# The head of an attention-plus-MLP kernel: two instead of three column blocks row tile by row tile, and the rows of query block 2 loaded earlier

## The chip, the cores and the metric

The kernel runs on one core of a Trainium2 chip. The metric is the device time of one execution, in microseconds (us), as the median of several runs.

## The reference, cut to what matters

```python
def reference(A_x, A_k_cache, A_v_cache, A_wq, A_wo, B_x, B_W_gate, B_W_up, B_W_down):
    x = A_x                                   # (1, 2048, 512) bf16
    xn = _layernorm(x, axis=-1)
    s = _A_ref(xn, A_k_cache, A_v_cache, A_wq, A_wo)          # 32 heads of attention, 2048 keys
    g = _silu(_B_ref(xn, B_W_gate, B_W_up, B_W_down))         # relu(xn Wg) * (xn Wu), then Wd
    return x + s * g
```

The branch with gate, up and down weights (512 x 1792, and back) is computed first, in four query blocks of 512 rows. Each block has 14 column blocks of 128 ("block 0" to "block 13" below) and then a down projection of four row tiles of 128 rows. The attention follows. The change touches only query block 0, at the very start.

## The kernel before: the parts that the change and the argument touch

The loads at the start are all issued from one queue, SP, except two:

```python
FCS = [0, 2, 5, 9, FC]          # weight pieces: blocks 0-1, 2-4, 5-8, 9-13
HFC = 3                         # blocks computed row tile by row tile
load_x0(sp, 0); load_x0(act, 1)                 # rows of query block 0, one tile each
load_w(sp, Wg_sb, wg_src, sem_wg, 0); load_w(act, Wu_sb, wu_src, sem_wu, 0)
load_x0(sp, 2); load_x0(sp, 3)
load_w(sp, Wg_sb, wg_src, sem_wg, 1); load_w(sp, Wu_sb, wu_src, sem_wu, 1)
load_xq(1)                                      # 512 rows of query block 1
load_w(sp, Wg_sb, wg_src, sem_wg, 2); load_w(sp, Wu_sb, wu_src, sem_wu, 2)
load_w(sp, Wg_sb, wg_src, sem_wg, 3); load_w(sp, Wu_sb, wu_src, sem_wu, 3)
for Q in range(2, QB):
    load_xq(Q)
sem_wd.sig(sp.dma_start(Wd_sb[:], ...))
```

(Statements are joined on lines here, to save room.) The head centres the rows on VectorE, transposes them on TensorE into PSUM, lets ScalarE copy them to `xcT`, and multiplies each row tile as soon as it is there. `head_tile(n, fc)` is eight matmuls of 128 columns: row tile n times gate and up weights of block fc.

```python
def head_ln():
    c0 = head_transpose(0, head_center(0))
    warm_mm(4)                       # matmuls on constants, no use made of them
    c1 = head_transpose(1, head_center(1))
    n2 = head_center(2)
    n3 = head_center(3)
    _wait(pe, c0)                    # c0..c3: the copy of that row tile is done
    head_tile(0, 0)
    head_tile(0, 1)
    _wait(pe, c1)
    head_tile(1, 0)
    head_tile(1, 1)
    c2 = head_transpose(2, n2)
    head_tile(0, 2)                  # these two run while ScalarE copies row tile 2
    head_tile(1, 2)
    _wait(pe, c2)
    head_tile(2, 0)
    c3 = head_transpose(3, n3)
    head_tile(2, 1)
    head_tile(2, 2)                  # and these two while it copies row tile 3
    _wait(pe, c3)
    for fc in range(HFC):
        head_tile(3, fc)
```

Blocks from HFC on use 512 columns, four matmuls for gate and four for up. The first of them uses the two accumulator banks; the others use a ring of three PSUM slots. A slot comes free when VectorE has multiplied gate and up. After each block of query block 0, VectorE and ScalarE also do one piece of the layernorm of later rows:

```python
def finish_gate_up(Q, fc, s, gtok, gu_tok):
    ...
    rtok = sem_relu.sig(act.activation(gr_sb[gk][:], g_ps, ACTF.Relu))
    _wait(dve, gu_tok); _wait(dve, rtok)
    h_tok = sem_h.sig(dve.tensor_tensor(hT[par][:, fc, :], gr_sb[gk][:], u_ps, ALU.mult))
    ...
    if Q == 0:
        ln_task(fc)     # fc 0-3: statistics of query block 1; 4-7: of block 2; 8-11: of block 3;
                        # 13: rstd of block 0, r2, r2h
```

So `ln_task(4)`, right after the multiply of block 4, needs the rows of query block 2. `r2h`, the last thing of that VectorE chain, is the scale of the first Tanh of the down projection, whose gate result frees the PSUM bank for row tile 2:

```python
_wait(act, ytok)                     # row tile j of the down projection is done
_wait(act, sig_free[jb])
if Q == 0 and j == 0:
    _wait(act, ln_hold["r2"])
stok = sem_sig.sig(act.activation(sig_sb[jb][:], ps_acc[:, jb, 0:D], ACTF.Tanh,
                                  scale=r2h[:, j, 0:1] if Q == 0 else 0.5))
```

The softmax here doesn't subtract the row's maximum and nothing guards it: scores larger than these inputs give would overflow.

## Time and profile before

| | before |
|---|---|
| median, lowest and highest of the first three runs | 1286.01 us, 1285.67 to 1286.48 |
| span in the profile | 1284.4 us |
| PE busy | 1279.1 us |
| first row-tile matmul of the head | 6.28 us |
| block 3 starts | 12.18 us |
| down projection of query block 0 starts | 31.70 us |
| first matmul of query block 1 | 44.03 us |

The last four are starts read from the timeline of the PE. From the profile's page, parts 1 and 4 (busy time with its share of the span and the number of instructions; then the chain of work that ended last, by engine):

```profile
PE 1279.1 (100%) x12050; PEld 836.4 (65%) x12050; DVE 380.5 (30%) x683; ACT 1002.2 (78%) x1111; POOL 13.2 (1%) x25
PE 98%; DVE 1%; ACT 0%; issue 0%; DMA 0%; ACTq 0%; DVEq 0%
```

TensorE bounds the kernel. The next view, the windows of the kernel before, shows where the little that is left lies. Its columns are the stretch, its length, then the busy time and number of instructions of each engine:

```profile
6.28:12.18 5.90, 5.90 (x108) 5.82 (x106) 2.21 (x7) 2.68 (x5) 0.00 (x0) 1.00 1.10 343
12.18:31.70 19.52, 19.15 (x91) 8.54 (x89) 16.12 (x40) 6.60 (x15) 6.03 (x8) 1.00 1.07 259
31.70:44.03 12.33, 12.26 (x58) 5.40 (x57) 6.45 (x14) 4.22 (x7) 6.25 (x8) 1.00 0.64 134
44.03:144.00 99.97, 99.97 (x465) 45.34 (x464) 37.35 (x55) 30.54 (x51) 0.00 (x0) 1.00 0.14 26
...
```

The first number after the length is PE's. PE is without a gap in the head, lacks 0.37 us in the second stretch and 0.07 us in the third, and has none from 44.03 to 144 us (nor, in a further window, from 144 to 1270 us: 1126.00 of 1126.00 us). The record of four wide matmuls lasts 1.03 us, though the next four start 0.86 us after them when nothing holds them: a busy record reaches 0.17 us too far, so the true losses are larger: from start to start 0.53 us and 0.24 us. Both come from waits. Of the list of waits of the kernel before, up to 44.03 us, four (total, times, longest):

```profile
DVE stats L313 <- DMA x_sb<-in_A_x_dram: 4.3, 2, 3.5
ACT L539 <- DVE r2h L449: 2.1, 1, 2.1
PEld ps_acc L531 <- DVE g_sb L548: 0.6, 1, 0.6
PE ps_r L508 <- DVE hT L473: 0.4, 1, 0.4
```

And the timeline around 20 us (start, duration, instruction, and in brackets the idle time before it and what ended it), first VectorE:

```profile
18.16 0.69 DVE L473 TENSOR_TENSOR hT<-gr_sb,ps_r 128x512 bf16<-128x512 bf16 x1 [0.92 <-ACT gr_sb L467]
19.62 0.69 DVE L313 BATCH_NORM_STATS2 stats<-x_sb 128x6 f32<-128x512 bf16 x1 [0.78 <-DMA x_sb<-in_A_x_dram]
...
20.51 0.69 DVE L473 TENSOR_TENSOR hT<-gr_sb,ps_r 128x512 bf16<-128x512 bf16 x1
```

then PE, at the head and at block 8:

```profile
8.07 0.39 PE L358 MATMUL ps_acc<-ident,xc_sb 128*128 128x128 bf16 x4
8.29 0.39 PE L410 MATMUL ps_r<-xcT,Wg_sb 128*128 128x128 bf16 x4
...
12.18 1.03 PE L508 MATMUL ps_acc<-xcT,Wg_sb 128*128 128x512 bf16 x4
13.04 1.03 PE L512 MATMUL ps_acc<-xcT,Wu_sb 128*128 128x512 bf16 x4
...
21.34 1.02 PE L508 MATMUL ps_r<-xcT,Wg_sb 128*128 128x512 bf16 x4 [0.37 <-DVE hT L473]
```

VectorE finishes the multiply of block 4 at 18.85 us and stands until the rows of query block 2 land, at 19.62. The multiply of block 5 therefore ends at 21.2 instead of about 20.4, and PE block 8, which needs that slot, starts at 21.34 instead of 20.81. Last, the chain of waits in order of time shows how the same VectorE chain goes on into the down projection:

```profile
34.12 0.50 DVE r2h L449
...
34.69 1.28 ACT L539
...
35.99 0.69 ACT sig_sb L539
...
37.23 0.70 DVE g_sb L548
...
37.97 1.04 PE ps_acc L531 x4
```

Row tile 2 of the down projection (37.97) starts only when the first gate result (37.93) has freed its bank, and the table load ahead of the first Tanh (34.69) waited for `r2h`.

### The profile page before, as it was taken

Reading aid. Unit: us, or ns where it says so; the run is one execution under the profiler, and the core shown is the slowest. Engines: PE = TensorE matmul, PEld = TensorE weight load, DVE = VectorE, ACT = ScalarE, POOL = GpSimd, SP = SyncE. Lnnn points to the kernel's source line nnn. Section 1 sums busy time; section 2 is a strip of 40 time slices with the busy share of each in tenths; the row PEclk is TensorE's granted clock in tenths of the full one; section 3 lists DMA queues with packets and bytes.
Section 4 is the critical chain, followed back from the end, with each engine's and each line's share of the span. In section 5 each row is a group of like instructions: output and inputs, shape, how many; then the busy total and the mean of one; then the engine's idle time right before and its main releaser. Section 6 shows DMA issues by size and latency. Waiting matters only on the chain.

```text
span 1284.4 us, 26956 instructions
## 1 busy us (share of the span) xinstructions
PE 1279.1 (100%) x12050; PEld 836.4 (65%) x12050; DVE 380.5 (30%) x683; ACT 1002.2 (78%) x1111; POOL 13.2 (1%) x25
## 2 busy tenths in 40 slices
PE   9999999999999999999999999999999999999998
PEld 5444466676666666666666666666666666666665
DVE  6433311112222222222222222222222222224355
ACT  3322399998888888888888888888888888888885
POOL 2100000000000000000000000000000000000000
PEclk9999999999999999999999999999999999999999
DMA  9600123332132332332322322233323322332212
GB/s 262 131 1 1 22 46 57 58 55 38 35 54 46 71 54 50 55 70 51 55 43 33 67 46 54 55 66 55 55 51 65 58 35 38 51 67 54 48 16 75
DMA packets 242033, 72.13 MB, mean 56 GB/s; under 512 B 227840, under 2 KB 241920, under 8 KB 241920
## 3 DMA queue, kind: packets, MB, share of 16 engines
q1 hardware_dynamic: 241248, 70.02, 29.6%
q8 instruction: 96, 1.57, 0.5%
q10 hardware_dynamic: 672, 0.39, 0.1%
q14 instruction: 17, 0.14, 0.0%
HBM read 32.77 MB, written 2.10 MB: 27 GB/s over the span
## 4 chain that ended last, share of the span: by engine, by line
PE 98%; DVE 1%; ACT 0%; issue 0%; DMA 0%; ACTq 0%; DVEq 0%
PE ps_acc L769 36%; PE ps_r L664 34%; PE ps_r L597 9%; PE ps_r L618 8%; PE ps_acc L531 3%; PE ps_r L508 3%; PE ps_r L512 3%; PE ps_r L803 1%; DVE stats L313 0%; PE ps_r L410 0%; DVE hT L473 0%; DMA x_sb<-in_A_x_dram 0%; DVE fin_tmp L811 0%; ACT gr_sb L467 0%; DVE x_sb L827 0%
## 5 line engine op out<-in xcount | busy, mean ns | idle before, releaser
L674 ACT ACTIVATE PT<-ps_r 128x1024 bf16<-128x1024 f32 x1024 | 952.5, 1054 | 167.7 <-PE ps_r L664 167.7
L769 PEld LDWEIGHTS ps_acc<-V_sb,PT 128*128 128x128 bf16 x8192 | 621.2, 98 | 241.9 <-ACT PT L674 3.5
L769 PE MATMUL ps_acc<-V_sb,PT 128*128 128x129 bf16 x8192 | 776.7, 220 | 0.0
L664 PE MATMUL ps_r<-QT_sb,KT_sb 128*128 128x512 bf16 x2048 | 754.1, 379 | 0.0
L691 DVE RECIPROCAL rz_sb<-ps_acc 128x4 f32<-128x4 f32 x127 | 23.3, 183 | 729.8 <-PE ps_acc L769 729.8
L664 PEld LDWEIGHTS ps_r<-QT_sb,KT_sb 128*128 128x128 bf16 x2048 | 195.0, 98 | 1.1 <-DVE QT_sb L608 0.4
L597 PE MATMUL ps_r<-xnT,Wq_sb 128*128 128x512 bf16 x512 | 130.9, 379 | 0.0
L618 PE MATMUL ps_r<-Wo_sb,OT_store 128*128 128x512 bf16 x448 | 114.6, 379 | 0.0
L608 DVE CAST QT_sb<-ps_r 128x512 bf16<-128x512 f32 x128 | 88.5, 692 | 48.1 <-PE ps_r L597 48.1
L597 PEld LDWEIGHTS ps_r<-xnT,Wq_sb 128*128 128x128 bf16 x512 | 49.9, 97 | 60.6 <-ACT PT L674 27.1
L694 DVE TENSOR_TENSOR Onorm<-ps_acc,rz_sb 128x512 bf16<-128x512 f32 x127 | 87.8, 691 | 4.4
L618 PEld LDWEIGHTS ps_r<-Wo_sb,OT_store 128*128 128x128 bf16 x448 | 43.8, 98 | 52.9 <-ACT PT L674 0.2
L631 DVE TENSOR_TENSOR s_acc<-s_acc,ps_r 128x512 f32<-128x512 f32 x96 | 66.0, 687 | 17.3 <-PE ps_r L618 17.3
L467 ACT ACTIVATE gr_sb<-ps_r 128x512 bf16<-128x512 f32 x55 | 32.2, 595 | 47.5 <-PE ps_r L508 47.0
L473 DVE TENSOR_TENSOR hT<-gr_sb,ps_r 128x512 bf16<-128x512 bf16 x55 | 37.7, 686 | 47.5 <-PE ps_r L512 41.2
L531 PE MATMUL ps_acc<-Wd_sb,hT 128*128 128x512 bf16 x224 | 49.2, 379 | 0.1
L508 PE MATMUL ps_r<-xnT,Wg_sb 128*128 128x512 bf16 x168 | 43.1, 379 | 0.0
L512 PE MATMUL ps_r<-xnT,Wu_sb 128*128 128x512 bf16 x168 | 43.1, 379 | 0.0
L531 PEld LDWEIGHTS ps_acc<-Wd_sb,hT 128*128 128x128 bf16 x224 | 21.8, 98 | 26.8 <-DVE g_sb L548 0.6
L539 ACT ACTIVATE sig_sb<-ps_acc 128x512 f32<-128x512 f32 x12 | 7.2, 597 | 29.5 <-PE ps_acc L531 29.5
L508 PEld LDWEIGHTS ps_r<-xnT,Wg_sb 128*128 128x128 bf16 x168 | 16.4, 98 | 19.8
L512 PEld LDWEIGHTS ps_r<-xnT,Wu_sb 128*128 128x128 bf16 x168 | 16.4, 98 | 19.8
(56 smaller groups left out, 184.7 us busy)
## 6 DMA issues: line engine op xcount, KB each, us to landing
V_sb<-in_A_v_cache_dram SPq DMA_DIRECT2D x32, 512.0 KB, 4.7
Wq_sb<-in_A_wq_dram SPq DMA_DIRECT2D x32, 128.0 KB, 2.5
Wo_sb<-in_A_wo_dram SPq DMA_DIRECT2D x8, 512.0 KB, 4.8
OT_store<-Onorm SPq DMA_TRANSPOSE x127, 2.5
Wd_sb<-in_B_W_down_dram SPq DMA_DIRECT2D x1, 1792.0 KB, 14.5
x_sb<-in_A_x_dram SPq DMA_DIRECT2D x3, 512.0 KB, 10.8
out_dram<-x_sb SPq DMA_DIRECT2D x6, 256.0 KB, 2.1
Wg_sb<-in_B_W_gate_dram SPq DMA_DIRECT2D x1, 640.0 KB, 10.3
```

The lines of the kernel that those rows point to most:

```text
L473: dve.tensor_tensor(hT[par][:, fc, :], gr_sb[gk][:], u_ps, ALU.mult)
L508: ins = pe.matmul(g_ps, Wg_sb[:, c, fs], xT[:, c, xs], start=(c == 0), stop=(c == DC - 1))
L512: ins = pe.matmul(u_ps, Wu_sb[:, c, fs], xT[:, c, xs], start=(c == 0), stop=(c == DC - 1))
L531: ins = pe.matmul(ps_acc[:, jb, 0:D], hT[par][:, fc, j * 128:(j + 1) * 128], Wd_sb[:, fc, :], start=(fc == 0), stop=(fc == FC - 1))
L597: ins = pe.matmul(ps_r[:, bank, :], Wq_sb[b][:, c, :], xnT[:, c, qs], start=(c == 0), stop=(c == DC - 1))
L608: etok = sem_qpe.sig(dve.tensor_copy(QT_sb[b][:, qs], ps_r[:, bank, :]))
L618: ins = pe.matmul(ps_r[:, bank, 0:D], OT_store[g % 2][:, hh, n * 128:(n + 1) * 128], Wo_sb[g % 2][:, hh, :], start=(hh == 0), stop=(hh == ...
L631: dve.tensor_tensor(s_acc[:, n, :], s_acc[:, n, :], ps_r[:, bank, 0:D], ALU.add)
L664: ins = pe.matmul(ps_r[:, 2 * s + tt, :], KT_sb[h % 2][:, t * 128:(t + 1) * 128], QT_sb[h % 2][:, qs], start=True, stop=True)
L674: act.activation(PT[pb][:], ps_r[:, 2 * s:2 * s + 2, :], ACTF.Exp, scale=scale)
L694: dve.tensor_tensor(Onorm[ob][:], o_ap, rz_sb[:].to_broadcast([128, 4, Dh]), ALU.mult))
L769: ins = pe.matmul(o_ap, PT[pb][:, tt, j * 128:(j + 1) * 128], V_sb[vb][:, t, 0:VW], start=(t == 0 and j % 2 == 0), stop=(t == KT - 1 and j ...
```

## The change

Its intent: run the third column block on all 512 rows at once, as the later ones, so that it needs fewer instructions and the row-by-row part is shorter; and bring the rows of query block 2 in before VectorE asks for them.

```diff
         FCS = [0, 2, 5, 9, FC]
-        HFC = 3
+        HFC = 2
...
         load_w(sp, Wg_sb, wg_src, sem_wg, 2)
         load_w(sp, Wu_sb, wu_src, sem_wu, 2)
+        load_xq(2)
         load_w(sp, Wg_sb, wg_src, sem_wg, 3)
         load_w(sp, Wu_sb, wu_src, sem_wu, 3)
-        for Q in range(2, QB):
+        for Q in range(3, QB):
             load_xq(Q)
...
             head_tile(1, 0)
+            c2 = head_transpose(2, n2)
             head_tile(1, 1)
-            c2 = head_transpose(2, n2)
-            head_tile(0, 2)
-            head_tile(1, 2)
             _wait(pe, c2)
             head_tile(2, 0)
             c3 = head_transpose(3, n3)
             head_tile(2, 1)
-            head_tile(2, 2)
             _wait(pe, c3)
-            for fc in range(HFC):
-                head_tile(3, fc)
+            head_tile(3, 0)
+            head_tile(3, 1)
```

## The prediction

> **What bounds the kernel.** TensorE. The page gives PE busy 1279.1 of 1284.4 us; the chain that ended last is 98% PE; granted clock 1.00. Windows: from 44.03 us to 1270 us PE has no idle time at all. The change touches only the first 44 us: head row tiles 6.28–12.18, gate/up blocks 3–13 of query block 0 12.18–31.70 (PE idle 0.37, start to start nearer 0.53), first down projection 31.70–44.03 (about 0.24 us lost at row tile 2). So at most about 1 us is to be won, under 0.1%.
>
> **Matmul cost removed.** 32 matmuls of 128 columns become 8 of 512. Timeline: four narrow ones start every 0.223 us (56 ns each), four wide every 0.864 us (216 ns). 1.79 us becomes 1.73: about 0.06 us won, nothing more. The Trainium skill, "TensorE: Matmul & The Clock Gate", the clock-gate part, gives start to start N ÷ 2.4 GHz plus 2.5 ns, 55.6 and 215.7 ns; the trace agrees.
>
> **What it adds.** Before, column block 2 of row tiles 0–2 filled the time while ScalarE copied the transposed rows (0.58 us, starting 0.42 us after the first transpose). Now one row-tile/block pair (0.45 us) follows each set of transposes, then PE waits for the copy. Adding up: transposes 2 at 7.62, copy ends 8.62, tile (2,0) 8.68 instead of 8.29; transposes 3 9.13, copy ends 10.13, tile (3,0) 10.19 instead of 9.80. Two new stalls of about 0.39 us. Block 2 starts at about 11.09, block 3 at 12.82 against 12.18: 0.64 us later.
>
> **What comes back.** (a) Block 0 is complete at about 10.6 instead of 11.26, so ScalarE and VectorE, which work off the backlog in 1.19 us per block, start 0.65 us earlier. (b) Rows of query block 2 landed at 19.6 us (issued 8.81, 10.8 us to landing) and the waits show VectorE idle 0.78 us for them; this held multiply 5 to 21.2 and PE block 8 from 20.81 to 21.34. Loaded before the last weight piece they land near 15. Multiply 5 then ends near 19.7, before block 8 needs the bank (21.45): stall gone, 0.53 us won. (c) The chain of waits runs over VectorE from 21 us to the factor r2h (34.62), which releases the Tanh table load (1.28 us) and then the first gate; that is why row tile 2 of the down projection waited. r2h moves to about 33.8, and this 0.24 us should vanish.
> The last weight pieces move by 512 KB at 347 GB/s, 1.5 us: landing near 19.6 (estimate), needed at 23.2. The same skill's "DMA: Bandwidth & Descriptors", queue order: each DMA engine consumes a ring's descriptors in order, so the earlier load really displaces the later; the landing times of before agree. Total bytes before rows 3 and the down weights are unchanged.
>
> **Sum.** +0.64 − 0.53 − 0.24 = −0.13 us at the end of the first down projection (about 43.9 instead of 44.03); everything later is the same PE stream. 1286.01 becomes 1285.9 us. Runs of one kernel spread 0.8 us, so 8 in 10: 1284.9 to 1287.0. Faster by 2%: 0.5%; within 2%: 99%; slower: 0.5%.
>
> **What would show it.** Timeline: row-tile matmuls of query block 0 in 8 groups of 8, with gaps near 8.3 and 9.8 us released by ScalarE's xcT copy; block 2 in the accumulator banks near 11.1; VectorE's stats no longer waiting for rows at 18.9; no PE gap at 21; down projection starting 31.7–31.9 and lasting 12.3 without the gap at row tile 2; first query-block-1 matmul near 43.9.
>
> **What would make it wrong.** The copies ending later than assumed, or the PE clock ramp falling differently (shifts the head by tenths); the late weight piece arriving after 23 us (PE stall at block 9); VectorE still late for r2h; drift of the chip between runs, which exceeds the effect.

## The result, and the profile after

| | before | after |
|---|---|---|
| median of 6 runs each | 1285.68 us (1285.48 to 1286.48) | 1285.82 us (1285.69 to 1285.97) |
| first row-tile matmul (F) | 6.28 | 6.47 |
| block 3 starts | 12.18 | 13.02 |
| down projection starts | 31.70 | 32.01 |
| first matmul of query block 1 (Q1) | 44.03 | 44.10 |
| rest, Q1 to the end of the span | 1240.4 | 1240.4 |

The ratio of the two times is 1.000 (95% interval 0.9987 to 1.0013). Ratios are the mean time of one kernel's fast runs over that of the other's of the same rounds, so not quite the ratio of the medians quoted. The interval is far wider than the effects here, so the traces have to tell them. They can, because everything after Q1 takes the same time.

The windows of the changed kernel, over the same stretches:

```profile
6.28:12.18 5.90, 5.44 (x82) 4.62 (x80) 2.60 (x8) 2.84 (x5) 0.00 (x0) 1.00 1.10 344
12.18:31.70 19.52, 19.52 (x92) 8.90 (x91) 16.11 (x41) 7.45 (x16) 6.03 (x8) 1.00 1.04 266
31.70:44.03 12.33, 12.33 (x59) 5.56 (x57) 5.68 (x14) 3.60 (x5) 6.26 (x8) 1.00 0.72 138
44.03:144.00 99.97, 99.97 (x465) 45.32 (x463) 37.25 (x55) 30.54 (x51) 0.00 (x0) 1.00 0.13 25
...
```

The gaps have moved: 0.46 us is missing in the head, and none in the two stretches after it. The waits say the same. Again four of the list, of the changed kernel up to 44.1 us:

```profile
DVE stats L314 <- DMA x_sb<-in_A_x_dram: 3.4, 1, 3.4
ACT L537 <- DVE r2h L447: 2.1, 1, 2.1
PEld ps_r L408 <- ACT xcT L364: 0.8, 2, 0.4
PE ps_r L408 <- ACT xcT L364: 0.5, 2, 0.2
```

Two waits of PE on ScalarE's copy are new. VectorE now waits for rows once (for the very first ones) and not twice, and from the first row-tile matmul on PE no longer waits for VectorE. ScalarE still waits 2.1 us for `r2h`, but this no longer reaches PE. In the timeline of the changed kernel, VectorE around 18 us:

```profile
17.72 0.69 DVE L471 TENSOR_TENSOR hT<-gr_sb,ps_r 128x512 bf16<-128x512 bf16 x1 [0.92 <-ACT gr_sb L465]
18.33 0.69 DVE L314 BATCH_NORM_STATS2 stats<-x_sb 128x6 f32<-128x512 bf16 x1
...
19.20 0.69 DVE L471 TENSOR_TENSOR hT<-gr_sb,ps_r 128x512 bf16<-128x512 bf16 x1
```

and PE in the head and at the end of the stage:

```profile
7.81 0.39 PE L359 MATMUL ps_acc<-ident,xc_sb 128*128 128x128 bf16 x4
...
8.25 0.39 PE L408 MATMUL ps_r<-xcT,Wu_sb 128*128 128x128 bf16 x4
8.87 0.40 PE L408 MATMUL ps_r<-xcT,Wg_sb 128*128 128x128 bf16 x4 [0.23 <-ACT xcT L364]
...
9.77 0.39 PE L408 MATMUL ps_r<-xcT,Wu_sb 128*128 128x128 bf16 x4
10.39 0.40 PE L408 MATMUL ps_r<-xcT,Wg_sb 128*128 128x128 bf16 x4 [0.23 <-ACT xcT L364]
...
11.29 1.03 PE L506 MATMUL ps_acc<-xcT,Wg_sb 128*128 128x512 bf16 x4
...
32.01 12.25 PE L529 MATMUL ps_acc<-Wd_sb,hT 128*128 128x512 bf16 x56
44.10 1.03 PE L506 MATMUL ps_r<-xnT,Wg_sb 128*128 128x512 bf16 x4
```

Four narrow matmuls start every 0.22 us; from 8.25 to 8.87 and from 9.77 to 10.39 it is 0.62. So each new stall costs 0.40 us. The chain that ended last no longer touches VectorE between 20 and 44 us; here, in order of time, the stretch that answers to the one shown of before:

```profile
30.88 0.43 PE ps_r L506 x2
31.31 0.86 PE ps_r L510 x4
32.18 6.91 PE ps_acc L529 x32
```

The rows of query block 2 were issued at 5.98 us and landed 9.9 us later, at 15.9. The last up-weight piece landed at 19.5 (issued 8.80, 10.7 us), well before block 9 at 23.4.

### The profile page after: what moved, and what is told of

The parts are those of the page before. It is cut to its first block, busy times and chain, and to the rows that moved or that the text cites. A ratio compares the mean times of both kernels' runs of the same rounds, so it can differ in the third digit from the quotient of the medians.

```text
span 1284.5 us, 26909 instructions
## 1 busy us (share of the span) xinstructions
PE 1279.5 (100%) x12026; PEld 836.1 (65%) x12026; DVE 380.1 (30%) x683; ACT 1002.5 (78%) x1111; POOL 13.2 (1%) x25
## 4 chain that ended last, share of the span: by engine, by line
PE 99%; DVE 0%; issue 0%; ACT 0%
PE ps_acc L767 36%; PE ps_r L662 34%; PE ps_r L595 9%; PE ps_r L616 8%; PE ps_acc L529 4%; PE ps_r L506 4%; PE ps_r L510 4%; PE ps_r L801 1%; PE ps_r L372 0%; PE ps_r L408 0%; DVE fin_tmp L809 0%; DVE x_sb L825 0%; PE ps_acc L359 0%; ACT xcT L364 0%; PE ps_acc L510 0%
## 6 DMA issues: line engine op xcount, KB each, us to landing
Wg_sb<-in_B_W_gate_dram SPq DMA_DIRECT2D x1, 640.0 KB, 10.1
```

## The experiments

The theory, in two paths that meet at Q1. **The row path**: the rows of query block 2 land at time L; VectorE's chain from there, over `r2h`, the table load and the first gate, sets when the down projection can go on. **The PE path**: PE's own matmuls and its stalls, counted from F. Q1 is the later of the two. The kernel before is on the row path with PE slack; the change brings the landing forward by 3.7 us (19.6 to 15.9), lengthens the PE path, and the kernel is now on that one. The row path as a whole has become only a little shorter, because most of the time won is filled by VectorE's and ScalarE's own work: `r2h` is complete at 33.99 us instead of 34.62, and the first gate at 37.30 instead of 37.93. That is about 0.75 us before PE wants to start row tile 2 (an estimate: 32.01 plus 28 matmuls of 0.216 us is 38.05). The main rival: PE bounds this kernel, so PE stalls count in full and VectorE's wait for rows does not count.

All times below are medians of five runs. The kernel before: its median was 1285.85 us for the first four experiments (rows only, head only, rows last, early transposes), 1285.61 for the next four (before again, the two delayed ones, third transpose early) and 1285.65 for the last four (Tanh without `r2h` and the three other repeats). The three calls ran on three different chips, so a time is compared with the kernel before of its own call where possible. All 95% intervals of the ratios include 1.

### Rows only

Three blocks row by row, as before, and only the load moved.

```diff
+        load_xq(2)
         load_w(sp, Wg_sb, wg_src, sem_wg, 3)
         load_w(sp, Wu_sb, wu_src, sem_wu, 3)
-        for Q in range(2, QB):
+        for Q in range(3, QB):
```

> Three column blocks row tile by row tile as before; only the rows of query block 2 load ahead of the last weight piece. Theory (two separate effects that add up with the order of waits): no head stalls, block 3 starts 5.90 us after the first row-tile matmul as before; VectorE does not wait for rows; no PE gap at block 8; r2h near 33.8, no gap at row tile 2 of the down projection. From the first row-tile matmul to the first matmul of query block 1: 37.0 us (before 37.75, changed kernel 37.63); time 0.77 us under before. Rival (the two parts of the change only do good together, the rows alone are off the critical path): 37.75 us, no change in time.

Measured: 1285.19 us, 0.66 below before; F 6.23, Q1 43.52, so 37.29 from one to the other. No gap at block 8, and the down projection took 12.09 us from start to start instead of 12.33. The missing 0.3 us against the expected 37.0 is a wait that I had not counted, at block 2 of row tile 0, for the second piece of the up weights. The timeline of PE in this run:

```profile
8.24 0.39 PE L411 MATMUL ps_r<-xcT,Wg_sb 128*128 128x128 bf16 x4
8.86 0.40 PE L411 MATMUL ps_r<-xcT,Wu_sb 128*128 128x128 bf16 x4 [0.23 <-DMA Wu_sb<-in_B_W_up_dram]
```

The start-to-start step is 0.62 instead of 0.22 us. In the kernel before it was 0.30 in the first trace and 0.77 in the second: this wait varies from run to run. The row path is close behind here: the first gate is ready at 37.30 us, about 0.18 us before PE needs it (estimated as above, 31.43 plus 28 matmuls), against 0.75 us in the changed kernel, where block 0 is complete earlier. The rival is out: the traces show that the rows alone bring a gain that the whole change did not (Q1 at 43.52 against 44.10); the times agree in their medians.

### Head only

The changed kernel with the loads in their old order.

```diff
-        load_xq(2)
         load_w(sp, Wg_sb, wg_src, sem_wg, 3)
         load_w(sp, Wu_sb, wu_src, sem_wu, 3)
-        for Q in range(3, QB):
+        for Q in range(2, QB):
```

> Two column blocks row tile by row tile, loads in the order of before. Theory: two head stalls of 0.39 us, block 3 starts 6.54 us after the first row-tile matmul; but they only take up time that PE later lost waiting for VectorE: VectorE still waits for the rows until 19.6 (about 1.3 us now, as it reaches them sooner), the PE gap at block 8 shrinks to nothing because PE comes later, r2h stays at 34.6 and a gap of about 0.1 us is left at row tile 2. First row-tile matmul to query block 1: 37.75 us, time within 0.1 us of before. Rival (PE is the bound, so a head stall is paid in full): 38.4 us, time 0.64 us above before.

Measured: 1285.75 us, 0.10 below before (within noise); both head stalls there, block 3 starts 6.56 us after F (12.63 and 6.07); VectorE waits 1.66 us for the rows, which land at 19.68; Q1 44.08. Counted from F, Q1 came after 38.01 us, not the 37.75 I had written. That yardstick was wrong: Q1 does not follow F here but the landing, 44.08 - 19.68 = 24.40, as in the kernel before, 44.03 - 19.62 = 24.41. The stalls of 0.8 us cost nothing in this kernel. The rival (0.64 us slower) is out. Two details missed: VectorE waited 1.66 us instead of 1.3, and from start to start PE still lost 0.14 us at block 8 and 0.24 at row tile 2, where nothing and 0.1 were expected.

### Rows of query block 2 last

The kernel before, with the suspected wait made longer.

```diff
-        for Q in range(2, QB):
+        for Q in reversed(range(2, QB)):
             load_xq(Q)
```

> Kernel before with the rows of query block 3 loaded ahead of those of query block 2, so that these land about 1.5 us later (21.1 instead of 19.6). Theory (PE block 8 and r2h hang on this landing): VectorE waits about 2.3 instead of 0.78 us, PE gap at block 8 about 2.0 us from start to start beyond the 1.73, first row-tile matmul to query block 1 39.2 us, time 1.5 us above before. Rival (the wait for the rows is not what held block 8): 37.75 us, no change.

Measured: 1287.23 us, 1.38 above before; ratio 1.001 with an interval from 0.9998 to 1.0023. VectorE, then PE in this run's timeline:

```profile
21.26 0.69 DVE L313 BATCH_NORM_STATS2 stats<-x_sb 128x6 f32<-128x512 bf16 x1 [2.31 <-DMA x_sb<-in_A_x_dram]
...
22.98 1.02 PE L508 MATMUL ps_r<-xcT,Wg_sb 128*128 128x512 bf16 x4 [1.90 <-DVE hT L473]
```

The rows landed 1.64 us later than in the trace of before, and Q1 came at 45.66, 1.63 us later: 24.40 after the landing again. The wait for the rows is what held the kernel before.

### Early transposes

The changed kernel with the transposes of row tiles 2 and 3 issued earlier, so that copies run under other tiles.

```diff
             _wait(pe, c1)
+            c2 = head_transpose(2, n2)
             head_tile(1, 0)
-            c2 = head_transpose(2, n2)
             head_tile(1, 1)
+            c3 = head_transpose(3, n3)
             _wait(pe, c2)
             head_tile(2, 0)
-            c3 = head_transpose(3, n3)
             head_tile(2, 1)
```

> The changed kernel with transposes 2 and 3 issued one row tile earlier, so that the copies run under row tiles 1 and 2. Theory: both head stalls go (at most 0.1 us waiting for VectorE's centred rows 3), block 3 starts 5.84 us after the first row-tile matmul, query block 1 36.9 us after it; time 0.8 us under before, 0.7 under the changed kernel, equal within 0.1 us to rows only. Rival (the narrower row-tile phase itself, not the copy wait, delays block 3): no better than the changed kernel.

Measured: 1285.13 us, 0.72 below before, its whole range (1284.99 to 1285.25) under that of before (1285.39 to 1286.78). No wait on the copies is left; block 3 starts 6.17 us after F (12.49 and 6.32) and Q1 37.25 after it, so 0.3 us more than expected. PE waited for VectorE's centred rows 2 instead: the transposes, now placed first, went off at 7.55 where about 7.21 was possible. About half of these 0.34 us is a late landing of the rows in this run (VectorE waited 0.17 us for it); the rest is VectorE's own time. The copy waits, not the 512-column form, were the cost in the head.

### Before and changed kernel, each with 0.43 us of useless PE work added

In both, four matmuls on constants, whose result nobody uses ("idle work" in the expectations), just ahead of the first row tile:

```diff
+            warm_mm(4)
             _wait(pe, c0)
             head_tile(0, 0)
```

On the kernel before:

> The kernel before with four more idle-work matmuls (0.43 us of PE) just ahead of the first row tile. Theory: the slack at block 8 takes them up. Block 3 starts 0.4 us later than before (about 12.6 to 12.8), the gap at block 8 shrinks to about 0.1 us, query block 1 still starts at 44.0 to 44.1, time within 0.1 us of before. Rival (PE is the bound, any PE work costs its time): 0.43 us above before.

Measured: 1285.61 us, the same as before (1285.61); F 6.73, rows landed 19.48, Q1 43.89, which is 24.41 after the landing. The matmuls took 0.44 us (6.29 to 6.73), and the gap at block 8 shrank to 0.03. The extra work cost nothing.

On the changed kernel:

> The changed kernel with the same four matmuls. Theory: with the wait for the rows gone PE has no slack, so all of it is paid: query block 1 starts 37.63 us after the first row-tile matmul, at about 44.4 to 44.5, time 0.3 to 0.45 us above the changed kernel (about 1286.2). Rival (the change left some slack on PE): under 0.15 us above the changed kernel.

Measured: 1286.17 us, 0.56 above before and 0.35 to 0.45 above the two medians of the changed kernel (1285.82, 1285.72); F 7.12, Q1 44.76, 37.64 after F. The matmuls took 0.49 us here (6.63 to 7.12), the rest of the later F is a later start. Q1 keeps its distance from F, so the extra work was paid in full in this trace; the interval of the times includes 1.

### Both kernels again, unchanged

> The kernel before, unchanged, for a second trace. Theory (from 21 us on it is paced by the landing of the rows of query block 2 and by VectorE, not by where the head starts): the first row-tile matmul may start anywhere between 6.0 and 6.5 us with the clock's ramp, but the PE gap at block 8 takes this up and the first matmul of query block 1 starts at 44.0 plus or minus 0.1 us. Rival (PE paces it): that start moves with the first row-tile matmul, 37.75 us after it.

Measured: 1285.72 us; F 5.99, L 19.66, Q1 44.06, which is 24.40 after L and 38.07 after F. F came 0.29 us earlier than in the first trace and Q1 did not move with it. But it was not the gap at block 8 that took this up, as expected. PE lost the lead, and more, at the wait for the up weights that rows only had met. The timeline of PE in this run:

```profile
8.00 0.39 PE L410 MATMUL ps_r<-xcT,Wg_sb 128*128 128x128 bf16 x4
8.77 0.40 PE L410 MATMUL ps_r<-xcT,Wu_sb 128*128 128x128 bf16 x4 [0.38 <-DMA Wu_sb<-in_B_W_up_dram]
...
21.38 1.02 PE L508 MATMUL ps_r<-xcT,Wg_sb 128*128 128x512 bf16 x4 [0.23 <-DVE hT L473]
```

The step of 0.77 instead of 0.22 us puts the start of block 3 at 12.35, 0.17 us later than in the first trace (the record of its first matmul is missing, so this is reckoned back from the next group, 13.21 - 0.86). The gap at block 8 shrank for that, from 0.53 to 0.40 us, and Q1 came 0.03 us later, with the landing 0.04 later. This still speaks for the landing as the pace, but by way of block 3 and not of F.

> The changed kernel, unchanged, for a second trace. Theory (PE paces it from the first row tile on): query block 1 starts 37.63 plus or minus 0.05 us after the first row-tile matmul, wherever that falls between 6.0 and 6.5 us. Rival: it starts at 44.1 whatever the head does, as in the two traces of before (44.03 and 44.06).

Measured: 1285.72 us against 1285.65 of before; F 6.49, Q1 44.12, 37.63 after F. It fits the theory, but both traces of the changed kernel have nearly the same F, so this one alone does not tell it from the rival; the delayed run does, with 37.64 at F 7.12.

### Tanh without r2h

The kernel before, with the constant 0.5 as the scale of the first Tanh group, and the wait for `r2h` gone with it. The result is wrong in the first 512 rows.

```diff
-                if Q == 0 and j == 0:
-                    _wait(act, ln_hold["r2"])
...
-                                   scale=r2h[:, j, 0:1] if Q == 0 else 0.5))
+                                   scale=0.5))
```

> The kernel before with the first Tanh group scaled by the constant 0.5 instead of r2h, so that neither it nor its table load waits for r2h; the result is wrong on purpose for the first 512 rows. Theory (r2h alone holds row tile 2 of the first down projection): the table load starts near 32.6 instead of 34.7 and is over when row tile 0 is done; the down projection takes 12.09 us instead of 12.33; the PE gap at block 8 stays; query block 1 starts at 43.8 instead of 44.0; time 0.24 us under before. Rival (the table load or the first gate itself, not r2h, holds it): 12.33 us and no change.

Measured: 1285.32 us, 0.33 below before. ScalarE in this run's timeline:

```profile
32.71 1.28 ACT L537 ACT_TABLE_LOAD   x1
35.05 0.60 ACT L537 ACTIVATE sig_sb<-ps_acc 128x512 f32<-128x512 f32 x1 [1.05 <-PE ps_acc L531]
```

The load is over 1 us before the Tanh needs it, and the Tanh now waits for PE. The down projection took 12.08 us; Q1 43.91 with L at 19.75, so 24.16 after the landing instead of 24.40. The 0.24 us at row tile 2 belong to the wait for `r2h`, with the table load behind it.

### Third transpose early, and rows only again

Early transposes had gained the copies and paid for centred rows. This one leaves the transposes of row tile 2 where the change put them and moves only those of row tile 3.

```diff
             head_tile(1, 1)
+            c3 = head_transpose(3, n3)
             _wait(pe, c2)
             head_tile(2, 0)
-            c3 = head_transpose(3, n3)
             head_tile(2, 1)
```

> The changed kernel with only the transposes of row tile 3 moved, to before the wait for the copy of row tile 2; those of row tile 2 stay where the change put them. Theory: of each 0.39 us stall only about 0.1 and 0.05 us are left, and the wait for VectorE's centred rows 2 that the early-transposes run had (0.34 us before its transposes 2) is not met. Block 2 starts 4.2 us after the first row-tile matmul (changed kernel 4.82, early transposes 4.45); query block 1 starts 36.95 to 37.05 us after it; time 0.6 to 0.7 us under the changed kernel and up to 0.2 us under rows only and early transposes, about 1285.1. Rival (nothing to be won in the head any more): equal to early transposes or slower.

Measured: 1285.08 us (1284.85 to 1286.31, one run out of line whose cause I don't know), 0.53 below before; F 6.15, Q1 43.17, 37.02 after F as expected. Run once more beside rows only, on one chip:

> Third transpose early, again: query block 1 starts 37.0 us after the first row-tile matmul; time 0.6 to 0.8 us under before and under the changed kernel, and 0 to 0.3 us under rows only, which waits for the up-weight piece at row tile 0. If its time comes out equal to rows only within 0.1 us, the wait for the weight piece is the only difference and falls away in most runs.

> Rows only, again, to stand beside the next run and the changed kernel on one chip: 0.6 to 0.8 us under before; query block 1 starts 36.98 us after the first row-tile matmul plus whatever PE waits for the second up-weight piece (0.3 us in its first trace).

Measured: third transpose early 1285.07 us, Q1 37.01 after F; rows only 1285.13 us, Q1 37.08 after F (the wait for the up weights was short this time). Both are 0.5 to 0.7 us under before (1285.65) and the changed kernel (1285.72) in their medians, and 0.06 us apart, which tells nothing between them. Third transpose early, rows only and early transposes are the fastest versions found; no interval is clear of 1.

## Why the prediction was right

The predicted time was 1285.9 us, the measured one 1285.82, inside 1284.9 to 1287.0, and "within 2%" held. Nearly any small change would have passed that, and part of the closeness is luck: the prediction started from 1286.01, and the median of the six runs of before is 1285.68. So the terms matter more. The first pair of traces is the one of before that the prediction was worked out from, with the first one of the changed kernel; the second pair is that of the repeats.

| term of the sum | predicted | first traces, before to after | second traces |
|---|---|---|---|
| head, F to block 3 | +0.64 | 5.90 to 6.55: +0.65 | 6.36 to 6.55: +0.19 |
| block 3 to the down projection (gap at block 8) | -0.53 | 19.52 to 18.99: -0.53 | 19.39 to 18.99: -0.40 |
| down projection to Q1 (`r2h`) | -0.24 | 12.33 to 12.09: -0.24 | 12.32 to 12.09: -0.23 |
| sum, F to Q1 | -0.13 | 37.75 to 37.63: -0.12 | 38.07 to 37.63: -0.44 |

Signs and mechanisms hold in both pairs. The agreement to a hundredth does not: it belongs to the trace that the prediction used. The head with three blocks takes 5.81 to 6.36 us from F to block 3 in its seven traces, because PE's wait for the second piece of the up weights goes from nothing to 0.55 us (0.08 us of it was in the trace used, unnamed); the new head takes 6.55 or 6.56 in all four of its traces, since it needs that piece later. In the kernel before, this variation costs nothing either, as the gap at block 8 changes with it.

- **The narrow against the wide matmuls.** "About 0.06 us won, nothing more" agrees with the step sizes in both traces: four narrow ones every 0.22 us, four wide every 0.86. This little gain is contained in the head's term.
- **Two head stalls of 0.39 us.** Measured 0.40 each, released by ScalarE's copy, where they were expected. Early transposes and third transpose early take these waits away and get back most of the 0.8 us from F to Q1 (37.25 and 37.02 against 37.63; the rest went into other waits), so the copy is the cause.
- **Rows landing near 15, last weight piece near 19.6.** They landed at 15.9 and 19.5. No stall at block 9. The prediction takes from the Trainium skill, "DMA: Bandwidth & Descriptors", Queues, rings and completion order, that a DMA engine consumes a ring's descriptors in order. The landings agree: the gate piece went from about 16.3 to 17.6 and the up piece from 18.1 to 19.5. But they were also issued that much later (6.00 to 7.54, 7.52 to 8.80), and from issue to landing they took nearly the same (10.3 and 10.1, 10.6 and 10.7 us), so no run here separates the order in the ring from the later issue.
- **Block 0 complete 0.65 us earlier.** ScalarE took up block 0 4.35 us after F instead of 4.98 (10.82 and 6.47, 11.26 and 6.28), 0.63 us earlier.
- **r2h and the table load.** Separated by the run without r2h, 0.24 us. `r2h` was complete at 33.99 us, predicted "about 33.8" for an F 0.19 us earlier.

What did not come out is the absolute step. The prediction said "about 43.9 instead of 44.03" and Q1 came at 44.10; the medians of the pooled runs differ by +0.14 us, and by +0.07 in the last call, instead of -0.1. That is the step from "F to Q1" to "us": the sum was added to the time of before as if both kernels hung on the same F. They do not. The kernel before hangs on L (24.40 to 24.41 us from L to Q1 in the five traces with late rows and `r2h` in use, with F from 5.99 to 6.73), the changed one on F (37.63 to 37.64 in three traces, one of them with the added work). So the sum of the three terms was right only for the one trace of before with its F of 6.28 and its short wait for the up weights; the changed kernel's F was 6.47 and 6.49. The prediction named this among its risks ("the PE clock ramp falling differently (shifts the head by tenths)") but did not carry it into the sum.

The first traces show the ramp itself, the rise of TensorE's speed in the first microseconds of its work. The timeline of PE just ahead of the head, kernel before:

```profile
4.93 0.38 PE L358 MATMUL ps_acc<-ident,xc_sb 128*128 128x128 bf16 x4 [0.16 <-DVE xc_sb L348]
5.15 0.61 PE L371 MATMUL ps_r<-const-bfloat16-1.0 128*128 128x256 bf16 x4
```

and changed kernel:

```profile
4.89 0.58 PE L359 MATMUL ps_acc<-ident,xc_sb 128*128 128x128 bf16 x4
5.27 1.06 PE L372 MATMUL ps_r<-const-bfloat16-1.0 128*128 128x256 bf16 x4
```

The same eight matmuls, which the change does not touch, took 1.5 to 1.7 times as long in the trace of the changed kernel, 0.58 for 0.38 and 1.06 for 0.61 us. It is not the change that does this: the run without `r2h`, whose head is that of before, had 0.58 and 0.91 us. The Trainium skill, "TensorE: Matmul & The Clock Gate", What's actually happening, says that the activity window which raises the clock is free-running, so that the transition varies between runs; the traces agree that it varies, the reason they don't show (the profile's granted clock reads 1.00 in the slow stretch too). In the second trace of the changed kernel the ramp was over in time (0.39 and 0.61 us) and F was late by another cause: the first centred rows were ready 0.24 us later than in its first trace. Over the twelve traces without added work F lies between 5.99 and 6.49 with a mean of 6.28. Whether the changed kernel has a later F on average, or its two traces and eleven runs fell so, stays open; nothing in its PE and VectorE instructions ahead of F differs.

Where the gain of the earlier rows went is thus shown: alone it is worth about 0.6 us (rows only, 0.66 and 0.52 in the medians), the new head alone costs nothing while the rows are late (head only), and together the head stalls, which had been free, are paid out of that gain.

## What to carry to other kernels

A stall is free only as long as another path ends later; when a change removes that other wait, look at which stalls on the remaining path it exposes, and test both halves of the change alone. Adding a small known delay to each version is a cheap test of slack: here 0.43 us of useless work cost nothing before, and its full length after. A stall that hangs on a landing varies from run to run (here the up weights, 0 to 0.55 us), so take it from several traces before it enters a sum. To read effects under a tenth of a per cent, measure between the event that paces the stage (here the landing of a load, or the first matmul) and its end, and not from the start of the program; if the two kernels are paced by different events, the variation of each event belongs into the predicted range.

## What the Trainium skill lacked or had wrong

- "TensorE: Matmul & The Clock Gate", Back-to-back issue gap: it gives about 81 ns (N = 128) and 131 ns (N = 512) per matmul for streams of weight load and matmul pairs, and calls the N ÷ 2.4 GHz + 2.5 ns form, which the prediction used, one for isolated matmuls. Here such streams run at that form: four narrow ones start every 0.22 to 0.23 us (56 ns each), four wide every 0.86 us (216 ns), with a weight load for each.
- "ScalarE: Activation LUTs", What ACT_TABLE_LOAD costs: the load's 1283 ns agrees with the 1.28 us here. The drain of about 1380 ns that it adds for every switch is not seen: in the kernel before the load starts at 34.69 us and the Tanh follows at 35.99, 0.02 us after the load's end; it was preceded by 2.12 us in which ScalarE waited for `r2h`, and in the run without r2h the load started 0.02 us after the Relu before it (32.11 + 0.58 to 32.71).
- No page that I read has it: how far the start of real work moves from run to run with the ramp and the landing of the first rows together, here 5.99 to 6.49 us over twelve traces.
